# k's first block ahead of x's second quarter, and the second sine table of each pair made from the first one's angles

## The chip, the core and the metric

The kernel runs on one core of a Trainium2 chip. A core has five engines, each with its own instruction queue that is worked off in order: PE (TensorE, matmuls and transposes into PSUM), DVE (VectorE, elementwise), ACT (ScalarE, functions and copies out of PSUM), POOL (GpSimd) and SP (SyncE, which here only issues transfers). They wait for each other through semaphores. Transfers (DMA) are issued by SP, ACT and POOL and run on 16 DMA engines that they share. The metric is the device time of one execution in microseconds.

## The reference, cut to what matters

Two independent halves share one output of 2048 rows. A: a sliding, dilated attention of 32 heads (window 8, dilation 2). B: a short shift filter over k of four taps, a product with v, a long convolution with a filter per channel, a gate with q.

```python
# A: x [2048, 576]
q, k, v = split(x @ wqkv)                  # 32 heads of 18
logits = q . k[pos - 2*w], w = 0..7        # masked where pos - 2*w < 0
o = softmax(logits * 18**-0.5) . v[pos - 2*w]
a = o @ wo
# B: q, k, v [2048, 576]
k_shift[s] = sum_t k_pad[s + t] * shift_k[:, 3 - t]      # k_pad: three zero rows, then k
kv = k_shift * v
y = irfft(rfft(kv, 2S) * rfft(ssm_k, 2S))[:S] + kv * ssm_D
b = q * y
out = concatenate([a, b], axis=-1)
```

## The kernel before, in words

The instructions stand in the program in an order written out by hand; no scheduler moves them. What is issued first on an engine runs first on it. Only the big part in the middle draws "units" of PE work from a list, and that list too is fixed when the program is built.

**Loads.** The order of the calls is the order on SP's queue: x's first quarter (`load_x(0)`, line 194), a third of wqkv for q (`load_w`, lines 154 and 156), x's second quarter (`load_x(1)`, line 194), k's first block of 512 rows (`load_k(0)`, lines 210 and 213), the third of wqkv for k, v's first block, k's second block, x's last two quarters by transposing transfers (`turn_x`), and so on. `load_k(0)` issues six transfers on SP: for rows 3 to 6 of the seven that a partition holds two by line 210 and one by line 213, then the same for rows 0 to 2. The first partition, which needs the three zero rows of the pad, is filled apart: a POOL memset of `kj[0:1, 0:3]` (line 205) and a POOL transfer of four rows (line 206).

**x turned.** The first two quarters of x lie with positions on the partitions and are transposed on PE (lines 467 and 472), then copied out of PSUM by ACT and DVE (lines 527, 528, 538, 477). `project_first(jp, ct0)` (line 494) projects q from quarter jp for two column tiles at a time: eight matmuls at line 500, two at line 502, one copy by ACT at line 504. PE's order around the change is: transposes of the first quarter, `spread_taps(256)`, `project_first(0, 0)`, transposes of the second quarter, `project_first(0, 2)`, `project_first(1, 0)`, `project_first(1, 2)`, then the units: projections of k (lines 378 and 389, copied by ACT at line 414) with folds of kv (line 606), transposes of sine tables (line 455) and others between. All the projections' PSUM tiles have the tag "A", of which there are two buffers: a projection may start when the copy of the one before the last is done.

**Sine tables.** The long convolution is done as products with cosines and sines. DVE makes integer angles: per table pair two multiply-adds (line 438) and one bitwise and (line 439), into `n_all`; ACT turns 1024 angles per partition into bf16 by one Sin (line 440). There are four such calls: `table_k(0)`, `table_k(1)` for the filter's transform (tile `TK`), `table_x(0)`, `table_x(1)` for kv's (tile `TX`). DVE makes the angles of k's two tables before the copies of x's first quarter (line 527), and those of x's two behind them. ACT's sines are placed apart, between the copies of projections:

```python
    project_first(0, 2)
    sines[2]()
    for n in range(2):
        project_first(1, 2 * n)
        sines[3 - 3 * n]()
```

and the fourth, `sines[1]`, behind the second unit (`with_sine`, line 554).

**Taps.** `taps(i)` (line 571) is DVE's work on block i: products of k's rows with the tap weights (line 577), sums (581), the product with v (597). For block 0 the first product reads rows 3 to 6 alone, the second rows 2 to 5. Each block's result is folded on PE (`mirror`, line 606). After the four blocks DVE makes the products of the logits (line 832), which PE sums (line 847) and ACT copies (line 852).

The tile `xw` begins with 512 columns of zeros (DVE memset, line 161) for PE's first idle matmuls (line 178); block 0's first tap product overwrites that place.

Of the kernel before, what the change touches and what calls it, by code (L numbers as in the profile page):

```python
# [11 lines left out]
ACT = mybir.ActivationFunctionType  # L12
ALU = mybir.AluOpType
FP32 = mybir.dt.float32
# [39 lines left out]
def view(t, offset, dims):  # L54

    return bass.AP(tensor=t.tensor, offset=t.offset + offset, ap=[list(t.ap[0])] + [list(d) for d in dims])
# [3 lines left out]
def kernel(  # L60
# [13 lines left out]
    nc = tc.nc  # L74
# [28 lines left out]
    HB = 4 * D  # L103
# [23 lines left out]
    xw = main.tile([128, 12 * HB], BF16, name="xw")  # L127
    XO = 8 * BL
    TB = main.tile([128, XO + 4 * BL], BF16, name="TB")
    TK = view(TB, 0, [[2 * BL, 2], [BL, 2], [1, BL]])  # L130
    TX = view(TB, XO, [[BL, 4], [1, BL]])
# [13 lines left out]
    def w_at(kb, comp):  # L145
        return HB * (9, 10, 5)[comp] + D * kb if kb < 4 else 11 * HB + D * (1, 2, 0)[comp]

    def wq(kb, comp, c0, n):
        return view(xw, w_at(kb, comp) + c0, [[1, n]])

    def load_w(eng, comp, to=None):
        low, high = (to[:, 0:4, :], to[:, 4, :]) if to is not None else \
            (view(xw, w_at(0, comp), [[D, 4], [1, D]]), wq(4, comp, 0, D))
        eng.dma_start(low, A_wqkv[0:512, comp * D:(comp + 1) * D].rearrange("(kb p) a -> p kb a", p=128))
        for r in range(2):
            eng.dma_start(high[64 * r:64 * r + 64, :], A_wqkv[512:576, comp * D:(comp + 1) * D])

    s1 = ExitStack()
    sp1 = s1.enter_context(tc.tile_pool(name="s1", bufs=1, reuse_waits="tile"))
    zeros = view(xw, 0, [[1, 512]])  # L160
    nc.vector.memset(zeros, 0.0)
    pib = main.tile([128, 1], FP32, name="pib")
# [3 lines left out]
    nc.scalar.dma_start(skrow[96:97, :], B_shift_k.rearrange("d j -> (d j)").unsqueeze(0))  # L166
    warm = sp1.tile([128, 1], FP32, name="warm")
    nc.scalar.activation(warm[:], pib[:], ACT.Sin)
    ones96 = sp1.tile([97, 256], BF16, name="ones96")
    nc.vector.memset(ones96[:], 0.0)  # L170
    nc.vector.memset(ones96[96:97, 0:128:2], 1.0)
# [10 lines left out]
    Ks = main.tile([128, 12 * HB], BF16, name="Ks")  # L182
    xnat = view(Ks, 4 * HB, [[HB, 4], [D, 4], [1, D]])
    n_all = view(Ks, 8 * HB, [[1, 4 * HB]]).bitcast(I32).rearrange("p (n f) -> p n f", n=9)
# [8 lines left out]
    def load_x(qtr):  # L193
        nc.sync.dma_start(xnat[:, qtr], xf[512 * qtr:512 * qtr + 512, :].rearrange("(sb p) c -> p sb c", p=128))
# [3 lines left out]
    def load_k(i):  # L198

        eng = nc.sync  # L200
        kj = sp1.tile([128, 7, D], BF16, name="kj", bufs=2)
        r0 = BL * i
        low = [(0, 64)]
        if i == 0:
            nc.gpsimd.memset(kj[0:1, 0:3, :], 0.0)
            nc.gpsimd.dma_start(kj[0:1, 3:7, :], kf[0:4, :].unsqueeze(0))
            low = [(1, 49), (49, 64)]
        for a, b in ((3, 7), (0, 3)) if i == 0 else ((0, 7),):
            for p0, p1 in low:
                eng.dma_start(kj[2 * p0:2 * p1:2, a:b], bass.AP(  # L210
                    tensor=kf.tensor, offset=kf.offset + (r0 + 4 * p0 - 3 + a) * D,
                    ap=[[4 * D, p1 - p0], [D, b - a], [1, D]]))
            eng.dma_start(kj[1:128:2, a:b], bass.AP(tensor=kf.tensor, offset=kf.offset + (r0 + 256 + 3 - a) * D,
                                                    ap=[[4 * D, 64], [-D, b - a], [1, D]]))
        kjs.append(kj)
# [15 lines left out]
    rp = main.tile([128, 8], FP32, name="rp")  # L231
# [10 lines left out]
                            base=0, channel_multiplier=-1)  # L242

    load_w(nc.sync, 0)
    load_x(1)

    def turn_x(h):
# [2 lines left out]
        nc.sync.dma_start(xnat[:, 2 + h, :, 512:576], xf[r0:r0 + 512, 512:576].rearrange("(sb p) c -> p sb c", p=128))  # L250
        nc.sync.dma_start_transpose(view(xw, 6 * HB + 512 * h, [[1024, 4], [1, 512]]), xf[r0:r0 + 512, 0:512])

    load_k(0)
    load_w(nc.sync, 1)
    load_v(0)
    load_k(1)
    turn_x(0)
    turn_x(1)
# [16 lines left out]
    for h in range(2):  # L275
        f = fold[:, 64 * h:64 * h + 64]
# [156 lines left out]
    nc.vector.tensor_copy(rp[:], rp_i[:])  # L433
    nc.vector.tensor_scalar(rp[64:128, 4:8], rp[64:128, 4:8], -510.0, None, op0=ALU.add)

    def table(n_i, T, vec, cols, period, offs):
        for n in range(2):
            nc.vector.tensor_scalar(n_i[:, n, :], vec, rp[:, cols[n]:cols[n] + 1], offs[n], op0=ALU.mult, op1=ALU.add)
        nc.vector.tensor_single_scalar(n_i, n_i, period - 1, ALU.bitwise_and)
        return lambda: nc.scalar.activation(T, n_i, ACT.Sin, bias=pib[:], scale=-2.0 * np.pi / period)  # L440

    def table_k(c):
        return table(n_all[:, 2 * c:2 * c + 2, :], TK[:, c, :, :], n_all[:, 8, :], (2 + c, 2 + c), 2048, (256.0, 1792.0))

    def table_x(n):
        return table(n_all[:, 4 + 2 * n:6 + 2 * n, :], TX[:, 2 * n:2 * n + 2, :], n_all[:, 8, :], (4, 5), 4096,
              (512.0 + 1024.0 * n,) * 2)

    def table_i(s):

# [28 lines left out]
    def pair_x():  # L479
        return pp.tile([128, 2, 1024], BF16, name="ps_x", tag="B")  # L480
# [13 lines left out]
    def project_first(jp, ct0):  # L494

        ps = bank2("ps_proj", "A")
        for e in range(2):
            c0 = 128 * (ct0 + e)
            for kb in range(4):
                nc.tensor.matmul(ps[:, e, :], wq(kb, 0, c0, 128), xT(kb, 512 * jp, 512), start=(kb == 0), stop=False)  # L500
        for e in range(2):
            nc.tensor.matmul(ps[:, e, :], wq(4, 0, 128 * (ct0 + e), 128)[64 * jp:64 * jp + 64],
                             x5(0)[64 * jp:64 * jp + 64], start=False, stop=True, tile_position=(64 * jp, 0))
        nc.scalar.activation(view(q, S * ct0 + 512 * jp, [[S, 2], [1, 512]]), ps[:], ACT.Copy)

    def spread_taps(n0):
        n = min(256, D - n0)
        ps = bank2("ps_sk", "A" if n == 256 else "B")
        for h in range(0, n, 128):
            w = min(128, n - h)  # L510
            sk = skrow[:, 4 * (n0 + h):4 * (n0 + h + w)].rearrange("p (d j) -> p d j", j=4)
            for r in range(2):
                nc.tensor.matmul(ps[:, h // 128, 0:4 * w], ones96[:, 128 * r:128 * r + 128],
                                 sk if r else view(skrow, 4 * (n0 + h) + 3, [[4, w], [-1, 4]]),
                                 start=(r == 0), stop=(r == 1))
        nc.scalar.activation(skb[:, :, n0:n0 + n],
                             ps[:].rearrange("p b (d j) -> p j (b d)", j=4)[:, :, 0:n], ACT.Copy)

    spread_taps(512)
    spread_taps(0)  # L520
    sines = [table_k(0), table_k(1)]
    pts = [pair_x() for _ in range(2)]
    for n in range(2):
        transpose_x(0, pts[n], 2 * n, range(4))
# [3 lines left out]
        nc.scalar.activation(xT(2 + n, 0, 512), pts[1][:, n, 0:512], ACT.Copy)  # L528
    copy_tail(0, pts[1])
    spread_taps(256)  # L530
    sines += [table_x(0), table_x(1)]
    project_first(0, 0)
    pts = [pair_x() for _ in range(2)]
    for n in range(2):
# [125 lines left out]
    def fold_filter(m):  # L660
        kt, swapped = kTok(m), m < 2

        def unit():
            assert m in signed
            minus = minus_of(m)
            pss = [bank2("ps_rev", "A") for _ in range(2)]
            for c in range(2):
                turns = [((flip2r, flip1)[c] if swapped else flip0, 1 - c), ((identn0, identn)[c], 2 + c)]
                if not swapped:
                    turns.insert(1, ((corner2, corner)[c], c))  # L670
                for n, (w, of) in enumerate(turns):
                    for h in range(2):
                        nc.tensor.matmul(pss[c][:, h, 0:HD], w[:], kt[:, of, HD * h:HD * h + HD], start=(n == 0),  # L673
                                         stop=(n == len(turns) - 1))
            for c in range(2):
                nc.scalar.activation(halves(kt[:, c, :]), pss[c][:, :, 0:HD], ACT.Copy, scale=0.5)
                pe(0.5, "A", 0.65)
            nc.gpsimd.dma_start(view(Ks, k_at(m, 2) + 2 * D, [[1, 2 * D]]), view(Ks, k_at(m, 2), [[1, 2 * D]]),
                                accum_op=ALU.add, max_dma_last_dim=2 * D)
            nc.gpsimd.dma_start(other(m)[1:128], kt[1:128, 0, :], accum_op=ALU.add)  # L680
            nc.gpsimd.dma_start(other(m)[0:1], minus, accum_op=ALU.add)

        return (1.0, unit, f"fold{m}")
# [21 lines left out]
    def made(f, *args):  # L705
        n = len(units)
        f(*args)
        return [units.pop() for _ in range(len(units) - n)][::-1]
# [13 lines left out]
    for i in range(NBL):  # L722
# [4 lines left out]
        if i < 2:  # L727
            load_k(i + 2)
            load_v(i + 2)
# [14 lines left out]
        if i == 3:  # L744
            need("fold3")
            first = made(filter_spectrum, 3)
            now = deque(first)
            first = [[now.popleft() for _ in range(min(n, len(now)))] for n in EARLY]
            now, first = first[0] + [fold_filter(2)] + first[1] + mirrors[:1] + first[2] + mirrors[1:], list(now)
# [3 lines left out]
        for n, u in enumerate(mirrors):  # L753
            n = AT[n] if n < 2 else AT[i]
# [591 lines left out]
```

## Time and profile before

| what | us |
|---|---|
| median of 3 runs | 212.61 |
| lowest and highest | 212.39 and 212.65 |
| the profiled execution | 212.5 |
| its span in the profile | 210.8 |

The profile shows one execution. Times within it count from the start of the span, which is 1.7 us shorter than the execution. A row of the timeline gives start, duration, engine, line, operation, what is written from what, and how many instructions were merged; in brackets stands how long the engine idled before and what ended the wait. SPq stands for an issue of a transfer on SP, PEld for a weight load. The chain of waits is the work that ended last, followed back from the end. In the slices a digit is the busy share in tenths of one fortieth of the span. A DMA's time to landing counts from its issue.

### The profile page before, as it was taken

The numbers are of one execution on the slowest core, as the hardware profiler recorded it, in microseconds if no ns is written. First come the engines' busy times: TensorE is split into PE (matmuls) and PEld (weight loads), VectorE is DVE, ScalarE is ACT, GpSimd is POOL, SyncE is SP. The second block draws the span as 40 slices with busy tenths as digits, with TensorE's granted clock in tenths as the row PEclk, the third lists the DMA queues.
The fourth block names the chain that finished last, engine by engine and source line by source line (L and its number), as shares of the span: only waits on it lengthen the run. The fifth ranks groups of instructions, "written<-read, shape, count | busy, mean of one in ns | idle before, by whom it ended". The sixth has DMA issues, their size and how long they took to land.

```text
span 210.8 us, 5106 instructions
## 1 busy us (share of the span) xinstructions
PE 200.1 (95%) x2114; PEld 110.7 (53%) x2122; DVE 193.1 (92%) x146; ACT 150.5 (71%) x218; POOL 74.0 (35%) x111
## 2 busy tenths in 40 slices
PE   7999999999999999899999999999989999999891
PEld 2443443344554656564354666656555666666460
DVE  7989999999999999858889999999999849999981
ACT  3799988657684989986369788855666796775540
POOL 8999993001195516320175000002029004033000
PEclk9999999999999999999999999999999999999999
DMA  6999998999639336999999997587559995985133
GB/s 201 303 328 231 266 342 280 170 192 182 151 75 122 48 40 87 180 181 171 235 225 238 194 234 159 105 208 185 153 223 255 239 322 110 214 243 182 28 113 111
DMA packets 35396, 39.66 MB, mean 188 GB/s; under 512 B 17619, under 2 KB 29007, under 8 KB 35374
## 3 DMA queue, kind: packets, MB, share of 16 engines
q1 hardware_dynamic: 26812, 24.88, 47.2%
q0 software_dynamic: 6096, 11.96, 30.4%
q10 hardware_dynamic: 2466, 2.51, 3.5%
q8 instruction: 16, 0.26, 0.5%
q14 instruction: 6, 0.05, 0.1%
HBM read 13.11 MB, written 4.72 MB: 85 GB/s over the span
## 4 chain that ended last, share of the span: by engine, by line
PE 80%; ACT 10%; DVE 5%; issue 2%; DVEq 0%; ACTq 0%
PE ps_proj L378 16%; PE ps_z L1126 9%; PE ps_wo L1029 8%; PE ps_acc L973 7%; PE ps_inv L1158 7%; PE ps_fx L776 6%; PE ps_log L847 4%; PE ps_proj L500 3%; PE ps_fk L627 3%; PE ps_proj L382 3%; PE ps_proj L389 3%; ACT Ks L695 3%; PE ps_rev L673 2%; PE ps_fk L628 1%; ACT qk L977 1%
## 5 line engine op out<-in xcount | busy, mean ns | idle before, releaser
L378 PE MATMUL ps_proj<-xw 128*128 128x512 bf16 x153 | 37.4, 380 | 0.6 <-issue 0.3
L832 DVE TENSOR_TENSOR av<-qk 128x4096 bf16<-128x4096 bf16 (+1 forms) x16 | 31.7, 2013 | 2.8 <-PE ps_log L847 2.8
L378 PEld LDWEIGHTS <-xw 128*128 128x128 bf16 x160 | 14.0, 97 | 20.5 <-issue 6.2
L1099 DVE TENSOR_TENSOR qk<-xw,Ks 128x2304 bf16<-128x2304 bf16 x14 | 18.5, 1355 | 2.5 <-PE ps_inv L1158 2.4
L1139 ACT ACTIVATE av<-ps_z 128x768 bf16<-128x768 f32 x20 | 15.3, 808 | 6.2 <-PE ps_z L1126 6.2
L414 ACT ACTIVATE qk<-ps_proj 128x1024 bf16<-128x1024 f32 x14 | 14.3, 1023 | 7.6 <-PE ps_proj L389 3.3
L695 ACT ACTIVATE Ks<-ps_fk 128x576 bf16<-128x576 f32 x32 | 18.6, 717 | 1.3 <-PE ps_fk L628 1.3
L577 DVE TENSOR_TENSOR tB<-kj,skb 128x4608 bf16<-128x4608 bf16 (+1 forms) x8 | 19.3, 2417 | 0.1
L778 ACT ACTIVATE xw<-ps_fx 128x576 bf16<-128x576 f32 x32 | 18.4, 666 | 0.0
L776 PE MATMUL ps_fx<-xw,TB 128*128 128x288 bf16 x128 | 18.0, 286 | 0.2
L1055 POOL DMA_DIRECT2D Ks<-Ks x3 | 3.7, 1218 | 41.1 <-PE ps_wo L1029 28.7
L1029 PE MATMUL ps_wo<-qk 128*128 128x288 bf16 x128 | 17.8, 287 | 0.0
L627 PE MATMUL ps_fk<-Ks,TB 128*128 128x384 bf16 x62 | 16.9, 326 | 0.8 <-ACT Ks L695 0.7
L414 ACT ACTIVATE v<-ps_proj 128x1024 bf16<-128x1024 f32 x9 | 9.3, 1029 | 9.3 <-PE ps_proj L378 4.3
L973 PE MATMUL ps_acc<-av,ident 64*64 64x512 bf16 x160 | 15.3, 377 | 0.0
L628 PE MATMUL ps_fk<-Ks,TB 128*128 128x192 bf16 x62 | 15.2, 245 | 0.0
L776 PEld LDWEIGHTS <-TB 128*128 128x128 bf16 x128 | 12.0, 97 | 6.0 <-issue 2.9
L1029 PEld LDWEIGHTS <-qk 128*128 128x128 bf16 x128 | 11.6, 98 | 5.6 <-issue 3.0
L1158 PE MATMUL ps_inv<-av,TI 128*128 128x288 bf16 (+1 forms) x96 | 13.6, 293 | 0.6 <-ACT av L1139 0.6
L1161 ACT ACTIVATE v<-ps_inv 128x576 bf16<-128x576 f32 (+1 forms) x14 | 9.5, 677 | 6.3 <-PE ps_inv L1158 6.3
L977 ACT ACTIVATE qk<-ps_acc 128x1024 bf16<-128x1024 f32 x8 | 8.2, 1024 | 8.0 <-PE ps_acc L973 8.0
L956 DVE TENSOR_TENSOR av<-Ks,v 128x4096 bf16<-128x4096 bf16 x6 | 13.6, 2286 | 0.2 <-PE ps_acc L973 0.2
(199 smaller groups left out, 471.3 us busy)
## 6 DMA issues: line engine op xcount, KB each, us to landing
Ks<-Ks POOLq DMA_DIRECT2D x9, 576.0 KB, 7.1
TB<-av SPq DMA_DIRECT2D x12, 256.0 KB, 5.5
kj<-in_B_k_dram SPq DMA_DIRECT2D x6, 504.0 KB, 6.1
vt<-in_B_v_dram SPq DMA_DIRECT2D x8, 288.0 KB, 5.2
Ks<-av SPq DMA_DIRECT2D x8, 256.0 KB, 5.5
Ks<-Ks SPq DMA_DIRECT2D x3, 576.0 KB, 6.1
Ks<-in_A_x_dram SPq DMA_DIRECT2D x2, 576.0 KB, 5.2
xw<-in_A_wqkv_dram SPq DMA_DIRECT2D x2, 576.0 KB, 5.9
```

What stands on the lines that cost most here:

```text
L378: nc.tensor.matmul(ps[:, jp, :], wq(kb, comp, 128 * ct, 128), xT(kb, 1024 * jj + 512 * jp, 512), **se)
L414: nc.scalar.activation(view(t, o + pad + 1024 * jj, [[512, 2], [1, 512]]), ps[:], ACT.Copy)
L577: dve(2304 * n, lambda: nc.vector.tensor_tensor(to, view(kj, row * D, [[D, n], [D, 4], [1, D]]), view(skb, row * D, [[D, n], [0, 4], [1, D ...
L627: nc.tensor.matmul(o[:, 0:2], w, rhs[:, 0:2], start=start, stop=stop)
L695: nc.scalar.activation(view(Ks, k_at(m, cs ^ (m & 1)) + 96 * gi, [[768, 3], [384, 2], [1, 96]]), acc3(ps), ACT.Copy, scale=(PSG, MSG)[cs][ ...
L776: nc.tensor.matmul(ps[:, pm, 0:HD], TX[:, 2 * pm + c, 128 * gi:128 * gi + 128], kv[:, 2 * c + pm, HD * h:HD * h + HD], start=(c == 0), sto ...
L832: return P, at, step, dve(1024 * nj, lambda: nc.vector.tensor_tensor(view(P, at, [[step, 4], [256, nj], [1, 256]]), view(t, o + 256 * hh, ...
L973: nc.tensor.matmul(acc[64 * o:64 * o + 64, h, :], ident[64 * h:64 * h + 64, 64 * h:64 * h + 64], view(P, 256 * u, [[2048, 2], [1, 256]])[6 ...
L1029: nc.tensor.matmul(ps[:, r, 0:HD], oT(hh, 2 * c + r, t)[:, o:o + 128], wo[:, t // 2, t % 2, HD * h:HD * h + HD], start=(t == 0 and h == 0) ...
L1099: r = dve(3 * QTR, lambda: nc.vector.tensor_tensor(pr, view(xw, HB * XG[i] + QTR * t, [[HB, 3], [1, QTR]]), view(Ks, k_at(j - i, 0) + QTR ...
L1126: nc.tensor.matmul(view(acc[r], 512 * h, [[192, 2], [96, 2], [1, 96]])[o:o + 64], w[64 * h:64 * h + 64, 64 * h:64 * h + 64], pr[64 * h:64 ...
L1158: nc.tensor.matmul(ps[:, c, 0:n], TI[:, sl, pm, 128 * c:128 * c + 128], Y(j, pm)[:, sl, c0:c0 + n], start=(pm == 0 and sl == 0), stop=(sl ...
```

## The change

Three edits. The call `load_k(0)` moves ahead of `load_x(1)`. Each pair of sine tables is made from one set of angles: ACT takes the Sin of the first table from the integer angles as before, then the absolute value of the same argument (Abs, into an fp32 place that the second table's integers had), and later the second table as the Sin of that value, scaled by plus or minus one and shifted by a quarter turn held in a new one-column tile. So DVE makes angles twice and not four times, and ACT does six calls and not four: `sines` now holds Sin and Abs of k's tables, the second Sin of k's, Sin and Abs of x's, the second Sin of x's, called at the same four places. And the three zero rows ahead of k are brought by a transfer on ACT's queue from the zeros in `xw` in place of a POOL memset.

```diff
+    quarter_turn = {}
+    for sign in (-1, 1):
+        quarter_turn[sign] = sp1.tile([128, 1], FP32, name="quarter_turn", bufs=2)
+        nc.gpsimd.memset(quarter_turn[sign][:], float(np.float32(-0.5 * sign * np.pi)))
...
         if i == 0:
-            nc.gpsimd.memset(kj[0:1, 0:3, :], 0.0)
+            nc.scalar.dma_start(kj[0:1, 0:3, :], view(xw[0:1], 0, [[0, 4], [1, 432]]))
             nc.gpsimd.dma_start(kj[0:1, 3:7, :], kf[0:4, :].unsqueeze(0))
...
     load_w(nc.sync, 0)
+    load_k(0)
     load_x(1)
...
-    load_k(0)
     load_w(nc.sync, 1)
...
-    def table(n_i, T, vec, cols, period, offs):
+    def table(at, cols, period, off, T, sign):
+        n_i = n_all[:, at:at + 2, :]
         for n in range(2):
-            nc.vector.tensor_scalar(n_i[:, n, :], vec, rp[:, cols[n]:cols[n] + 1], offs[n], op0=ALU.mult, op1=ALU.add)
+            nc.vector.tensor_scalar(n_i[:, n, :], n_all[:, 8, :], rp[:, cols + n:cols + n + 1], off, op0=ALU.mult,
+                                    op1=ALU.add)
         nc.vector.tensor_single_scalar(n_i, n_i, period - 1, ALU.bitwise_and)
-        return lambda: nc.scalar.activation(T, n_i, ACT.Sin, bias=pib[:], scale=-2.0 * np.pi / period)
...
+        mag = view(Ks, 8 * HB, [[1, 4 * HB]]).bitcast(FP32).rearrange("p (n f) -> p n f", n=9)[:, at + 2:at + 4, :]
+
+        def first():
+            nc.scalar.activation(T[0], n_i, ACT.Sin, bias=pib[:], scale=-2.0 * np.pi / period)
+            nc.scalar.activation(mag, n_i, ACT.Abs, bias=pib[:], scale=-2.0 * np.pi / period)
+
+        def second():
+            nc.scalar.activation(T[1], mag, ACT.Sin, bias=quarter_turn[sign][:], scale=float(sign))
+
+        return [first, second]
+
+    def table_k():
+        return table(0, 2, 2048, 256.0, [TK[:, :, n, :] for n in range(2)], -1)
+
+    def table_x():
+        return table(4, 4, 4096, 512.0, [TX[:, 2 * n:2 * n + 2, :] for n in range(2)], 1)
...
-    sines = [table_k(0), table_k(1)]
+    sines = table_k()
...
-    sines += [table_x(0), table_x(1)]
+    sines += table_x()
```

More of the change, by code (lines that the diff above doesn't have):

```diff
@@ L434 @@
     nc.vector.tensor_scalar(rp[64:128, 4:8], rp[64:128, 4:8], -510.0, None, op0=ALU.add)
-    def table(n_i, T, vec, cols, period, offs):
+    def table(at, cols, period, off, T, sign):
+        n_i = n_all[:, at:at + 2, :]
         for n in range(2):
-            nc.vector.tensor_scalar(n_i[:, n, :], vec, rp[:, cols[n]:cols[n] + 1], offs[n], op0=ALU.mult, op1=ALU.add)
+            nc.vector.tensor_scalar(n_i[:, n, :], n_all[:, 8, :], rp[:, cols + n:cols + n + 1], off, op0=ALU.mult,
+                                    op1=ALU.add)
         nc.vector.tensor_single_scalar(n_i, n_i, period - 1, ALU.bitwise_and)
[L440 to L447, printed above, removed]
+        mag = view(Ks, 8 * HB, [[1, 4 * HB]]).bitcast(FP32).rearrange("p (n f) -> p n f", n=9)[:, at + 2:at + 4, :]
[9 more added lines that the diff above has]
+        return table(4, 4, 4096, 512.0, [TX[:, 2 * n:2 * n + 2, :] for n in range(2)], 1)
     def table_i(s):
```

## The prediction

> **What bounds the kernel now.** I read the page's busy times, slices and chain first, then the chain in order of time, then the waits of DVE, then the timelines of SP, PE, DVE and ACT up to 26 us, where all of the change lies.
>
> ```profile
> PE 200.1 (95%) x2114; PEld 110.7 (53%) x2122; DVE 193.1 (92%) x146; ACT 150.5 (71%) x218; POOL 74.0 (35%) x111
> ...
> PE   7999999999999999899999999999989999999891
> ...
> DVE  7989999999999999858889999999999849999981
> ...
> PE 80%; ACT 10%; DVE 5%; issue 2%; DVEq 0%; ACTq 0%
> ```
>
> Two engines look full, and the chain decides between them: 80% of it is PE, 5% DVE. The slices say where DVE gives way. It is full up to the sixteenth and then drops to 5 to 8 tenths, while PE stays at 9 but for one 8. Ten microseconds at a time (columns: PE, PEld, DVE, ACT, POOL), and DVE's longest wait:
>
> ```profile
> 80.00:90.00 10.00, 9.24 (x80) 5.75 (x82) 8.82 (x7) 10.00 (x17) 4.63 (x5) 1.00 0.90 146
> 90.00:100.00 10.00, 9.84 (x84) 5.32 (x78) 7.20 (x5) 7.59 (x13) 1.17 (x1) 1.00 1.02 175
> 100.00:110.00 10.00, 9.84 (x75) 4.01 (x75) 8.65 (x6) 4.86 (x5) 4.81 (x9) 1.00 0.95 228
> ```
>
> ```profile
> DVE av L832 <- PE ps_log L847: 2.8, 3, 1.4
> ```
>
> Between 80 and 110 us DVE idles 1.2 + 2.8 + 1.4 = 5.3 us, and its longest wait there is for PE's sums of the logits. So a few microseconds won on DVE before 80 us only lengthen that wait, and the time follows PE, whose instructions stand in one fixed order. In the first 26 us PE meets two edges, and the change touches both.
>
> **First part: the order of the loads.** load_k(0) issues six transfers on SP, one on POOL and, now, one on ACT. Between the old and the new place of the call POOL and ACT issue nothing, so only SP's order changes: the six pass one transfer, x's second quarter.
>
> ```profile
> 3.13 0.59 SPq L194 DMA_DIRECT2D Ks<-in_A_x_dram  x1
> 3.76 1.54 SPq L210 DMA_DIRECT2D kj<-in_B_k_dram  x2
> 5.35 0.73 SPq L213 DMA_DIRECT2D kj<-in_B_k_dram  x1
> 6.12 1.58 SPq L210 DMA_DIRECT2D kj<-in_B_k_dram  x2
> 7.75 0.66 SPq L213 DMA_DIRECT2D kj<-in_B_k_dram  x1
> 8.46 0.60 SPq L154 DMA_DIRECT2D xw<-in_A_wqkv_dram  x1
> ```
>
> The six begin at 3.76 and the next load at 8.46: 4.70 us of SP. The quarter, now issued at 3.13, is issued at 3.13 + 4.70 = 7.83. The transfers from line 194 and from line 213 took, from issue to landing:
>
> ```profile
> DMA to landing us min/median/max: 4.2/5.2/6.2
> ...
> DMA to landing us min/median/max: 5.1/6.3/6.9
> ```
>
> ```profile
> 7.80 1.91 PE L500 MATMUL ps_proj<-xw 128*128 128x512 bf16 x8 [0.35 <-DVE xw L527]
> 9.65 0.60 PE L502 MATMUL ps_proj<-xw 64*128 64x512 bf16 x2
> 10.18 1.07 PE L467 MATMUL ps_x<-ident,Ks 128*128 128x128 bf16 x16
> ...
> 11.88 1.36 DVE L577 TENSOR_TENSOR xw<-kj,skb 128x2304 bf16<-128x2304 bf16 x1 [0.72 <-DMA kj<-in_B_k_dram]
> ...
> 13.15 1.36 DVE L577 TENSOR_TENSOR tB<-kj,skb 128x2304 bf16<-128x2304 bf16 x1
> ```
>
> The quarter has landed by 3.13 + 6.2 = 9.33 today, 0.85 us ahead of its transposes at 10.18. When does it land in its new place? By the two transfers of line 194, between 7.83 + 4.2 = 12.0 and 7.83 + 6.2 = 14.0. The nearest row is another: k's last piece is today the eleventh transfer of SP, issued at 7.75, behind the same bytes that the quarter will have ahead of and in it. It landed no earlier than 7.75 + 5.1 = 12.85 (the shortest of its line), and by 13.24, when the second tap product, which reads it, follows the first (11.88 + 1.36) without a wait. I take 13.05. PE has nothing else in its order: the second pair of first projections stands behind the transposes. So PE starts them at 13.05 in place of 10.18: **2.87 us later**, with bounds of 1.8 and 3.8. ACT's copies of the transposed quarter, and all behind them, move by as much.
>
> In exchange k lands earlier by about the quarter's share of the queue, some 2 us: the first tap product starts near 10 in place of 11.88. That is a gain for DVE, which the wait of the 90s takes back: nothing.
>
> **Second part: the sine tables.** DVE loses two of the four tables:
>
> ```profile
> L438 DVE TENSOR_SCALAR Ks<-Ks,rp 128x512 int32<-128x512 int32 x8 | 3.6, 494 | 0.0
> ...
> L439 DVE TENSOR_SCALAR Ks<-Ks 128x1024 int32<-128x1024 int32 x4 | 2.8, 709 | 0.1
> ...
> L440 ACT ACTIVATE TB<-Ks,pib 128x1024 bf16<-128x1024 int32 x4 | 4.6, 1140 | 0.0
> ```
>
> Half of 3.6 + 2.8 is 3.2 us less on DVE before 11.1. Without it the taps would still wait for k. What it reaches on PE is the start of the first projection, which waited 0.35 us for a DVE copy at 7.80; those 0.35 us end in the wait for x's quarter: nothing. ACT keeps its four sines and gains two Abs of 128x1024, one behind the first sine and one behind the third. The trace has no Abs. Its nearest row is the sine of the same shape and input, 1.14 us; the cheapest of this size is a copy at 1.02. ACT is full at this place:
>
> ```profile
> 14.21 1.02 ACT L504 ACTIVATE qk<-ps_proj 128x1024 bf16<-128x1024 f32 x1
> 15.13 1.14 ACT L440 ACTIVATE TB<-Ks,pib 128x1024 bf16<-128x1024 int32 x1
> 16.36 1.02 ACT L504 ACTIVATE qk<-ps_proj 128x1024 bf16<-128x1024 f32 x1
> 17.28 1.14 ACT L440 ACTIVATE TB<-Ks,pib 128x1024 bf16<-128x1024 int32 x1
> 18.73 1.02 ACT L504 ACTIVATE qk<-ps_proj 128x1024 bf16<-128x1024 f32 x1 [0.30 <-PE ps_proj L502]
> 19.65 1.14 ACT L440 ACTIVATE TB<-Ks,pib 128x1024 bf16<-128x1024 int32 x1
> 20.89 1.02 ACT L414 ACTIVATE qk<-ps_proj 128x1024 bf16<-128x1024 f32 x1
> 21.81 1.14 ACT L440 ACTIVATE TB<-Ks,pib 128x1024 bf16<-128x1024 int32 x1
> 22.93 1.02 ACT L414 ACTIVATE qk<-ps_proj 128x1024 bf16<-128x1024 f32 x1
> ```
>
> ```profile
> 22.95 1.01 ACT qk L414
> ...
> 24.00 0.38 PE ps_proj L378
> ```
>
> From start to start a sine takes 1.12 us where nothing lies between (21.81 to 22.93). So the slack behind the first three sines is 16.36 - 16.25 = 0.11, then 18.73 - 18.40 = 0.33, then 20.89 - 20.77 = 0.12, in all 0.56 us. Two Abs at 1.12 are 2.24; less the slack, the copy at 22.93 comes 1.68 us later. The last two rows, from the chain, show who waits: PE's projection at 24.00 starts when that copy (22.95 + 1.01) has emptied its PSUM buffer. PE therefore loses **1.68 us** a second time. Bounds: at a copy's pitch of 0.92 (14.21 to 15.13) 1.84 - 0.56 = 1.28; with no overlap and no slack 2 x 1.14 = 2.28. Both losses add, since ACT's row as a whole moves with the transposes.
>
> The trace shows no load of another function table beside the sines. [...]
>
> **Third part: k's pad by a transfer.** POOL loses a memset and gains two of one column; ACT gains one issue.
>
> ```profile
> L205 POOL MEMSET kj<- 1x1728 bf16 x1 | 1.5, 1529 | 0.0
> ...
> 3.62 0.38 ACT L516 ACTIVATE skb<-ps_sk 128x256 bf16<-128x256 f32 x1 [0.73 <-PE ps_sk L513]
> ```
>
> POOL is 1.5 us ahead; no engine above waits for it. ACT's issue stands where ACT idles 0.73 us before 3.62, and what it reads, DVE's zeros, is long there. An issue of 0.5 to 0.9 us, as SP's rows show, fits or comes 0.2 us late to a copy that leads to the taps alone: nothing. Its landing, at most 6.2 us on, is before 10. If it came later only DVE's first products would wait.
>
> **The sum.** 2.87 + 1.68 = 4.55 us on PE before 29 us, with no part of it given back that the chain shows: it stays on PE or on ACT behind PE. The profiled execution took 212.5 us (span 210.8, 1.7 around it), the median is 212.61. 212.5 + 4.55 = 217.05, with the 0.1 to the median **217.1 us**. From the bounds alone: 1.8 + 1.28 gives 215.7, 3.8 + 2.28 gives 218.7.
>
> **The rivals.** (1) *The quarter lands in time all the same*, since transfers share 16 engines and mine treats them as a queue: ACT's term alone, 212.6 + 1.7 = 214.3. Against it: no transfer of these lines lands in under 4.2 us. 8%. (2) *The Abs hide*, in the wait for x: 212.6 + 2.9 = 215.5. Against it: ACT's order puts them behind the copies of that x. 12%. (3) *PE's clock falls* during the wait. The row that prices it:
>
> ```profile
> L178 PE MATMUL ps_idle<-xw 128*128 128x512 bf16 x4 | 1.9, 627 | 1.3 <-DVE pib L163 1.3
> ...
> 5.08 1.06 PE L467 MATMUL ps_x<-ident,Ks 128*128 128x128 bf16 x16
> ```
>
> The first matmuls took 1.9 / 4 = 0.47 us each, where eight of that shape took 1.91 at 7.80; the transposes at 5.08 are as fast as those at 10.18 (1.06 and 1.07). So PE started at half speed and was full by 5.08, at most 3.8 us on. Going through that again would cost half of 3.8: 217.1 + 1.9 = 219.0. The wait of 3.1 us (from 9.65 + 0.60 - 0.35 = 9.9 to 13.05) is the first long one behind it; the trace has no such wait to show what the clock does. [...] 10%. (4) *The Abs bring table loads*, one before and one behind each: four at the 1.28 us of
>
> ```profile
> L168 ACT ACT_TABLE_LOAD x1 | 1.3, 1283 | 1.4 <-PEq L1330 1.4
> ```
>
> add 5.1: 222.2. 3%. (5) *Faster: DVE is the bound after all.* From 11.88 to 80 us DVE has hardly a wait, so its 1.9 us of earlier taps would pass through to the end: 210.7. It decides only if x's quarter lands by 10.2, so that PE stays ahead, and if the logits' products then hold up the sums and not the reverse. The waits of the 90s speak against it. 4%. (6) *All of it hides*, within 0.2%: 3%.
>
> **How the numbers follow.** The forecast of both terms has 60%. Slower by over 0.2% (0.4 us, about what a measurement of this kernel can tell from no change) are the forecast and rivals 1 to 4: 0.93; within it 0.03; faster 0.04. The range from 214.2 to 219.1 takes in rivals 1 to 3 and the bounds, and leaves out some 13 in 100: rivals 4 to 6 and a tail.
>
> **What would show it.** Step one: the transposes of x's second quarter start near 13 with a wait for the transfer of x, and the tap products near 10. Step two: Abs rows of about 1.1 us, and PE waiting for a copy of line 414's kind near 28.5. Sum: the sums of the logits and all behind them later by 4 to 5 us, DVE's idle time before 110 us longer by 5 or more. I am wrong if the transposes start before 12, if PE's wait at the second edge is missing, or if PE makes the loss good where DVE now leads.

## The result, and the profile after

The changed kernel takes 217.91 us (median of 4 runs, 217.13 to 221.53) against 212.55 us before; the ratio is 1.0246, 95% interval 1.0219 to 1.0274. The run of 221.53, whose mean granted clock was 0.94, is not in the ratio; without it the median is 217.25. The profiled execution took 217.25 us, 4.75 more than the one profiled before, its span is 215.5 against 210.8.

The page of the changed kernel, the same parts as shown of before:

```profile
PE 201.9 (94%) x2114; PEld 112.2 (52%) x2122; DVE 189.4 (88%) x140; ACT 152.1 (71%) x220; POOL 68.2 (32%) x112
...
PE   7959989999999999989999999999989999999891
...
DVE  6599999999952999966889999999999959899982
...
PE 76%; ACT 13%; DMA 5%; issue 2%; DVE 1%; SPq 1%; DVEq 0%; ACTq 0%
```

DVE has 3.7 us less work and a new hole in its twelfth and thirteenth slice (5 and 2 tenths). PE has a hole in its third (5), and a transfer now stands in the chain with 5%. PE's instructions are as many as before, yet it is busy 1.8 us *longer*, which the diff does not explain. Here are PE's timeline at the first hole, SP's issues ahead of it, and the time to landing of line 198, the loads of x:

```profile
9.76 0.60 PE L516 MATMUL ps_proj<-xw 64*128 64x512 bf16 x2
12.89 1.59 PE L481 MATMUL ps_x<-ident,Ks 128*128 128x128 bf16 x16 [2.53 <-DMA Ks<-in_A_x_dram]
...
15.80 1.89 PE L514 MATMUL ps_proj<-xw 128*128 128x512 bf16 x6 [0.22 <-issue]
17.63 0.60 PE L516 MATMUL ps_proj<-xw 64*128 64x512 bf16 x2
```

```profile
5.61 2.22 SPq L214 DMA_DIRECT2D kj<-in_B_k_dram  x2
7.88 0.66 SPq L217 DMA_DIRECT2D kj<-in_B_k_dram  x1
8.59 0.60 SPq L198 DMA_DIRECT2D Ks<-in_A_x_dram  x1
```

```profile
DMA to landing us min/median/max: 4.2/4.2/4.3
```

PE waits 2.53 us for x's second quarter and starts on it at 12.89, 2.71 us later than before. Then it is slow: the 16 transposes take 1.59 us (1.07 before), and the last two matmuls of the projection start at 17.63 where before they started at 13.36, so 2.71 has become 4.27. The granted clock (the third number from the right in a row of one microsecond, before the DMA share and the GB/s) says why:

```profile
13.00:14.00 1.00, 1.00 (x14) 1.00 (x14) 1.00 (x1) 0.00 (x0) 1.00 (x1) 0.63 1.10 384
14.00:15.00 1.00, 1.00 (x10) 0.63 (x8) 0.96 (x2) 0.00 (x0) 1.00 (x2) 0.50 1.05 333
15.00:16.00 1.00, 0.78 (x3) 0.41 (x4) 1.00 (x1) 0.92 (x1) 1.00 (x1) 0.50 1.20 371
16.00:17.00 1.00, 1.00 (x4) 0.36 (x3) 0.96 (x2) 1.00 (x2) 0.94 (x2) 0.66 0.96 381
17.00:18.00 1.00, 1.00 (x6) 0.21 (x3) 0.99 (x1) 0.61 (x2) 1.00 (x1) 1.00 0.95 341
```

It falls to one half at about 13.26 (0.26 at full and 0.74 at half speed make 0.63) and is back at 16.68. The wait is the first loss and the clock the second. The third is the place where PE waits for ACT ("ACT's edge" below). These are ACT's sine, Abs and copy, then the copy that PE needs, and PE itself:

```profile
19.19 1.14 ACT L449 ACTIVATE TB<-Ks,pib 128x1024 bf16<-128x1024 int32 x1
20.23 1.14 ACT L450 ACTIVATE Ks<-Ks,pib 128x1024 f32<-128x1024 int32 x1
21.27 1.01 ACT L518 ACTIVATE qk<-ps_proj 128x1024 bf16<-128x1024 f32 x1
...
28.14 1.03 ACT L418 ACTIVATE qk<-ps_proj 128x1024 bf16<-128x1024 f32 x1
```

```profile
29.22 1.02 PE L382 MATMUL ps_proj<-xw 128*128 128x512 bf16 x3 [0.99 <-ACT qk L418]
```

An Abs takes 1.14 us, 1.04 from start to start. PE waits 0.99 us for the copy, and its third unit starts at 29.22 in place of 24.00: 5.22 late. From there PE keeps that distance: each of its sums of the logits, products with v and inverse transforms starts 5.20 or 5.21 us later than before, up to what stood at 194 us. DVE's rows, the first from before, the others from the changed kernel:

```profile
56.70 4.47 DVE L832 TENSOR_TENSOR av<-qk 128x4096 bf16<-128x4096 bf16 x2
```

```profile
9.97 1.36 DVE L591 TENSOR_TENSOR xw<-kj,skb 128x2304 bf16<-128x2304 bf16 x1 [1.51 <-DMA kj<-in_B_k_dram]
...
54.95 4.47 DVE L846 TENSOR_TENSOR av<-qk 128x4096 bf16<-128x4096 bf16 x2
...
68.82 3.43 DVE L846 TENSOR_TENSOR av<-qk 128x4096 bf16<-128x4096 bf16 x2 [6.76 <-ACT v L418]
```

The taps begin at 9.97 (11.88 before), the products of the logits at 54.95 (56.70 before), and then DVE waits 6.76 us for ACT's copy of what PE projected late. Its lead is wholly given back there; up to 110 us DVE is busy 8.3 us less than before, of which 3.7 are work that it no longer has. Only at the very end is something won back. The chain before, then after:

```profile
192.13 1.12 issue
193.25 0.91 DVE qk L1099
194.16 0.36 issue
```

```profile
200.17 1.10 PE ps_z L1140 x24
201.27 0.02 issue
201.29 0.82 ACT av L1153
```

Before, the last stage of PE stood for a moment behind DVE; now DVE comes in time, and the distance falls from 5.21 to 4.80.

### The profile page after: what moved, and what is told of

Same layout as the page of the kernel before. It is cut to its first block, busy times and chain, and to the rows that moved or that the text cites. A ratio compares the mean times of both kernels' runs of the same rounds, so it can differ in the third digit from the quotient of the medians.

```text
span 215.5 us, 5105 instructions
## 1 busy us (share of the span) xinstructions
PE 201.9 (94%) x2114; PEld 112.2 (52%) x2122; DVE 189.4 (88%) x140; ACT 152.1 (71%) x220; POOL 68.2 (32%) x112
## 4 chain that ended last, share of the span: by engine, by line
PE 76%; ACT 13%; DMA 5%; issue 2%; DVE 1%; SPq 1%; DVEq 0%; ACTq 0%
PE ps_proj L382 15%; PE ps_z L1140 9%; PE ps_wo L1043 8%; PE ps_inv L1172 7%; PE ps_acc L987 7%; PE ps_fx L790 6%; PE ps_log L861 4%; PE ps_fk L641 3%; DMA xw<-in_A_wqkv_dram 3%; ACT Ks L709 3%; PE ps_proj L386 3%; PE ps_proj L393 2%; DMA Ks<-in_A_x_dram 2%; PE ps_rev L687 2%; PE ps_fk L642 1%
```

## The experiments

**Theory:** PE sets the time, and loses it in three places: by the wait for x (load order), by the clock that falls during or behind that wait, and by ACT's edge (the Abs). **Rivals:** the tables or the transfers alone carry the loss; DVE sets the time; PE was slow because transfers disturb it, not by its clock.

**The load order alone.** The kernel before, with

```diff
     load_w(nc.sync, 0)
+    load_k(0)
     load_x(1)
```

and the old call taken out.

> The kernel before with the load order of the changed one alone (k's first block ahead of x's second quarter; tables and pad as before). Theory (PE waits for x's quarter, then runs at half clock for a while): the transposes of x's second quarter start at 12.6 to 12.9 in place of 10.18, the tap products near 10; PE's projections of the units are 4.0 to 4.4 us later where the clock falls and 2.5 to 2.8 where it does not, the wait before the copy of line 414 near 24 adds under 0.2. Time 216.2, between 214.8 and 216.8. Rival (the tables carry the loss): 212.6 to 213.5.

216.1 us (median of 4; 214.73, 216.0, 216.19, 216.31) against 212.38, ratio 1.0163 [1.0136, 1.0190]. The median is as expected; the profiled run is the one at 214.73:

```profile
12.80 1.07 PE L467 MATMUL ps_x<-ident,Ks 128*128 128x128 bf16 x16 [2.55 <-DMA Ks<-in_A_x_dram]
...
26.62 1.89 PE L378 MATMUL ps_proj<-xw 128*128 128x512 bf16 x7
```

The wait is there (2.55 us), the transposes are fast, and the third unit is 2.62 late. So the same wait does not always cost the clock. The three other runs left no profile, so the same kernel was run once more.

> The new load order alone once more, for a second profile. Theory: if the time is near 216.1, the granted clock is under 1.00 for some 3.4 us from 12.9 to 14 us on, the matmuls of the projection behind the transposes take twice as long, and the units are 4.0 to 4.2 us later than before; if the time is near 214.7 the clock is 1.00 throughout and the units are 2.6 us later. Rival: near 216.1 with a clock of 1.00.

216.38 us in one run, and this profile shows the fall:

```profile
12.79 1.07 PE L467 MATMUL ps_x<-ident,Ks 128*128 128x128 bf16 x16 [2.02 <-DMA Ks<-in_A_x_dram]
...
14.13 3.57 PE L500 MATMUL ps_proj<-xw 128*128 128x512 bf16 x8
```

```profile
14.00:15.00 1.00, 1.00 (x7) 0.37 (x5) 1.00 (x1) 0.76 (x1) 0.99 (x1) 0.60 1.01 272
15.00:16.00 1.00, 1.00 (x4) 0.39 (x3) 0.97 (x2) 1.00 (x2) 0.89 (x3) 0.50 1.19 422
16.00:17.00 1.00, 1.00 (x3) 0.30 (x2) 1.00 (x1) 0.77 (x2) 1.00 (x1) 0.50 0.94 370
17.00:18.00 1.00, 1.00 (x4) 0.11 (x2) 0.96 (x2) 0.00 (x0) 0.93 (x2) 0.69 1.00 337
```

The transposes start at the same place (12.79 and 12.80) and take 1.07 us in both. Here the clock falls at 14.2, behind them, and the eight matmuls of the projection take 3.57 us in place of 1.90. The units' first projection starts at 22.91 here and at 21.24 there, 1.67 us apart, for 1.65 between the two times.

**The wait filled.** If the clock falls because PE idles, giving it work must stop that. Eleven matmuls whose result nobody reads, in the changed kernel and in the kernel with the order alone:

```diff
     project_first(0, 0)
+    ps = bank2("ps_idle", "A")
+    for _ in range(11):
+        nc.tensor.matmul(ps[:, 0, :], wq(0, 0, 0, 128), wq(0, 0, 0, 512), start=True, stop=True)
```

> The changed kernel with 11 matmuls of 512 columns on q's weights, whose result nobody reads, between the first projection and the transposes of x's second quarter: PE is busy in place of idle while it waits. Theory (the wait lets PE's clock fall): granted clock 1.00 in 13 to 17 us, the 16 transposes in 1.07 us in place of 1.59, the eight matmuls of the projection behind them in 1.9 in place of 2.7; ACT's edge behind takes back 0.2 of the 1.56. Time 215.9, between 215.5 and 216.4. Rival (PE is slow there since the transfers disturb its reads): no change against the changed kernel, 217.2.

215.94 us (215.91 to 216.10), ratio 1.0171 [1.0155, 1.0186]: the useless work makes the changed kernel over a microsecond faster, and its runs agree within 0.2 us. The transposes take 1.07 us again, and ACT's edge takes back its part, 1.20 us:

```profile
12.83 1.07 PE L481 MATMUL ps_x<-ident,Ks 128*128 128x128 bf16 x16 [0.62 <-DMA Ks<-in_A_x_dram]
...
27.81 1.89 PE L382 MATMUL ps_proj<-xw 128*128 128x512 bf16 x7 [1.20 <-ACT qk L418]
```

> The kernel before with the new load order alone, and 11 matmuls of 512 columns on q's weights between the first projection and the transposes of x's second quarter. With the order alone the profiled execution kept its full clock through a wait of 2.55 us and took 214.73 us, while the three other runs took 216.0 to 216.3. Theory (in those runs the clock fell in the wait): with PE busy all runs lie near 214.7, between 214.4 and 215.0, without the runs at 216. Rival (the 1.4 us come from elsewhere, such as the transfers): runs at both levels as before, median 216.1.

214.87 us (214.56 to 215.00), ratio 1.0101 [1.0057, 1.0145]: no run at 216 any more. The transposes still start at 12.88, for x comes no earlier and the transfers are the same ones; only PE's idling is gone, and with it the slow matmuls. So a disturbance by the transfers is out as the cause.

**The tables alone.** The kernel before with the new `table` and its calls; loads and pad as before.

> The kernel before with the new sine tables alone (load order and pad as before). Theory (ACT is full between 14 and 23 us, two Abs of 1.04 each less the slack of some 0.9): PE's projection of the third unit starts 0.9 to 1.3 us late, less 0.3 won where the first projection no longer waits for DVE's copy. Time 213.2, between 212.8 and 213.6. Rival A (the Abs hide): 212.3. Rival B (DVE is the bound, and 3.2 us less on it shorten the kernel): under 211.5.

213.29 us (212.69 to 214.0, 8 runs), ratio 1.0043 [1.0027, 1.0059]: slower, though DVE is busy 2.9 us less (190.2 for 193.1). PE's wait at the third unit is 1.21 us:

```profile
25.22 1.89 PE L382 MATMUL ps_proj<-xw 128*128 128x512 bf16 x7 [1.21 <-ACT qk L418]
```

**The Abs twice.** The same, with

```diff
             nc.scalar.activation(mag, n_i, ACT.Abs, bias=pib[:], scale=-2.0 * np.pi / period)
+            nc.scalar.activation(mag, n_i, ACT.Abs, bias=pib[:], scale=-2.0 * np.pi / period)
```

> The kernel before with the new sine tables, and each of the two Abs issued twice (same result). Theory (ACT sets PE's pace here with no slack left): two more Abs of 1.04 us come through in full, PE's wait before the third unit is 1.2 + 2.1 = 3.3 us, time 213.3 + 2.1 = 215.4, between 215.0 and 215.8; more by up to 1.5 if PE's clock falls in that wait. Rival (the loss of the tables lies elsewhere, such as the strided table or DVE): 213.3 as with one.

215.38 us (215.08 to 217.2), ratio 1.0161 [1.0127, 1.0196]; 2.1 us over one Abs each, as expected. PE's waits for ACT's copies up to 40 us:

```profile
PE ps_proj L382 <- ACT qk L418: 1.3, 1, 1.3
...
PE ps_ti L470 <- ACT qk L418: 1.2, 1, 1.2
PE ps_proj L382 <- ACT qk L519: 0.8, 1, 0.8
```

They sum to 3.3 us, 2.1 over the 1.2 of one Abs. There is no slack left on ACT at this place: what is added comes through whole.

**The pad alone.**

```diff
-            nc.gpsimd.memset(kj[0:1, 0:3, :], 0.0)
+            nc.scalar.dma_start(kj[0:1, 0:3, :], view(xw[0:1], 0, [[0, 4], [1, 432]]))
```

> The kernel before with k's pad by a transfer alone. Theory: DVE's cast of line 433, 1.07 us beside POOL's memset, falls to 0.1, so the copies of x's first quarter and the first projection start 0.3 us earlier, which PE keeps: 212.3, between 212.0 and 212.6. SP's fourth transfer of k waits for q's weights, as in the changed kernel (7.0 us), so what follows on SP is 0.5 to 1 us later and costs nothing. Rival (the later issues reach PE): 213.0 or more.

212.44 us (212.19 to 214.49, 12 runs), ratio 1.0003 [0.9979, 1.0027]: no difference that these runs show. PE does get its start, and loses it:

```profile
7.35 1.89 PE L500 MATMUL ps_proj<-xw 128*128 128x512 bf16 x8
...
22.90 0.68 PE L606 MATMUL ps_fold<-xw,fold 128*64 128x288 bf16 x8 [0.48 <-DVE xw L597]
```

It begins the first projection 0.45 us earlier and at 22.90 waits 0.48 us for block 0's product on DVE. So DVE, though not the bound, stands right behind PE there.

> The kernel before with the pad by a transfer, and the two folds of block 0 one pair of units later on PE. With the pad alone PE ran 0.46 us ahead from 7.4 us on and lost it at 22.9, waiting 0.48 us for DVE's product that the first fold reads. Theory: with the fold behind the next projection PE keeps its lead; 0.3 to 0.46 us less than before: 212.0, between 211.9 and 212.3. Rival (the lead is lost at the next edge, ACT's copies, or by the fold's copies coming late): no change, 212.4.

Pad by transfer and `n = AT[n] + 2 * (i == 0) if n < 2 else AT[i]`, so that the fold comes a pair of units later: 212.61 us (212.05 to 214.61, 12 runs) against 212.25, ratio 1.0015 [0.9994, 1.0035]. The wait for DVE is gone; in its place PE waits for ACT:

```profile
5.11 1.90 PE L467 MATMUL ps_x<-ident,Ks 128*128 128x128 bf16 x16
...
30.82 1.46 PE L378 MATMUL ps_proj<-xw 128*128 128x512 bf16 x6 [0.49 <-ACT TI L459]
```

The rival's edge is there. The first row shows an execution whose clock rose late (1.90 us for transposes that take 1.07 at full clock), so this profile cannot say how much of the lead lived until 30.8; the runs show no gain. No version here beats the kernel before.

**PE's own work in the wait.** In the changed kernel, `project_first(0, 2)` ahead of the transposes of x's second quarter.

> The changed kernel with the second pair of first projections ahead of the transposes of x's second quarter, so that PE has 2.37 us of its own work where it waited. Theory: PE waits under 0.7 us for x's quarter and its clock stays full, but the projection behind the transposes now waits for ACT's two copies of the quarter (1.94 us), so 1 to 2 us of the loss come back in another place; ACT's edge adds 0.5 to 1. Time 215.0, between 214.0 and 216.0. Rival A (the wait for x is the whole of the loss): 213.4. Rival B (order on PE makes no difference): 217.2.

215.58 us (215.09 to 216.4), ratio 1.0157 [1.0132, 1.0182], within the theory's range and off in one part:

```profile
12.87 1.07 PE L481 MATMUL ps_x<-ident,Ks 128*128 128x128 bf16 x16 [0.69 <-DMA Ks<-in_A_x_dram]
...
15.39 3.63 PE L514 MATMUL ps_proj<-xw 128*128 128x512 bf16 x8 [1.11 <-ACT xw L553]
```

The wait for x shrinks to 0.69 us and, as expected, 1.11 us come back as a wait for ACT's copies of the quarter. The expectation that the clock would stay full was wrong: it fell at 15.5, just behind the second of these two waits, and the projection took 3.63 us in place of 1.9. This profiled execution, at 216.4 us, is the slowest of the four.

## Why the prediction was right, point by point

- **What bounds the kernel.** Right. DVE started its logits 1.75 us earlier and then waited 6.76 us; PE's delay of 5.2 us passed through 165 us of the kernel unchanged.
- **x's second quarter.** Right in its result: transposes at 12.89 for a forecast of 13.05, 2.71 us for 2.87. The way there was a little different: it was issued at 8.59 and not at 7.83, since SP waited 0.8 us, until 7.02, for the load of q's weights. With the order alone, where the pad is a memset, SP does not stand there and issues the quarter at 7.74; with the pad alone it does. PE could start at nearly the same time either way (12.80 and 12.89), so the time of issue did not set the landing. That the bytes ahead of it did, as the choice of the nearest row assumed, fits both; no run varied them alone.
- **The Abs.** Mechanism right, size too high: 1.68 forecast, 1.20 and 1.21 measured with the clock full, 0.99 in the changed kernel, where ACT's copies came only 4.06 us later (18.27 for 14.21) and PE 4.27, which is 0.21 us more of slack. The step that failed took the sine's pitch as 1.12 from the starts at 21.81 and 22.93, "where nothing lies between". The copy at 22.93 had waited for PE, whose matmuls ended at 22.89. The pitch is 1.04 in the changed kernel. With it the four gaps between sine and copy in the rows of before are 0.19, 0.41, 0.20 and 0.08, in all 0.88 us, and 2.08 - 0.88 is the 1.20 that was measured. No table was loaded around the Abs: in the changed kernel an Abs follows its sine after 1.04 us, and the trace has two table loads of 1.28 us, at 1.40 and 38.46 us (before: at 1.39 and 33.31), none of them between the first sine at 19.19 and the last at 27.10.
- **The clock.** This was a rival at 10% and it happened in the profiled execution, and probably in the other two at 217.13 and 218.56, whose mean granted clocks are no higher (0.989 and 0.984, for 0.990). It cost 4.27 - 2.71 = 1.56 us, for a price of 1.9. So a loss that the forecast left out of its sum was there. The 10% was the author's estimate: the trace of before, in which PE waits 1.3 us at most, could not show what a longer wait does. In the changed kernel PE idled 2.53 us and the clock fell (more below).
- **The sum.** 4.55 us forecast, 4.75 measured in the profiled execution, by errors that cancel: 0.16 too much for the load, 0.69 too much for the Abs, 1.56 missed for the clock, and 0.41 given back at the end, where "no part of it given back" was wrong. (These four make 4.85; the 0.1 that is left lies in PE's gaps and behind its last matmul.) Two of the three losses were foreseen with their mechanism; that the total came so close, without the third, is luck. By the ratio the loss is 5.2 us.
- **The pad at nothing.** Right for this kernel, for half the reason: POOL's memset did cost something, since DVE's small cast (line 433, 437 after the change) took 1.07 us beside it and takes 0.10 in the changed kernel. PE's 0.45 us behind that are real but lost again at the first fold. In the changed kernel they do not show, since its clock rose late and the first projection started at 7.94, behind the 7.80 of before.

## What to carry to other kernels

An engine with a fixed order pays for a late input at once, and for good when it is the bound: here PE paid 2.71 us for x's quarter. The lead of 1.75 us that DVE won, an engine that waits for it, was worth nothing. Work moved to an engine that is full just there costs its duration less the gaps at that place (1.20 of 2.08 us for the first two Abs, all of the next two), however much slack that engine has over the whole span, so weigh it in the stage where it lands. When taking a pitch from two starts, first see whether the second instruction was waiting for someone.

## What the runs showed of the hardware

PE's clock fell after waits shorter than the time for which it then stayed low, and not always after the same wait. It fell after 2.53 us of idle time in the changed kernel, after 2.02 us in the second run of the load order, and after 0.69 and 1.11 us close together in the kernel with the projections swapped. It did not fall after 2.55 us in the first run of the load order, nor after 0.62 us with the wait filled.

The granted clock was one half from 13.26 to 16.68 us in the changed kernel, from 14.2 to 17.6 in the second run of the load order, and from 15.5 to 18.9 with the projections swapped, 3.4 us each time. The rows of the last:

```profile
15.00:16.00 1.00, 0.61 (x2) 0.25 (x2) 1.00 (x1) 1.00 (x2) 1.00 (x1) 0.76 1.22 358
16.00:17.00 1.00, 1.00 (x3) 0.25 (x2) 0.97 (x2) 0.95 (x3) 1.00 (x2) 0.50 0.98 380
17.00:18.00 1.00, 1.00 (x4) 0.33 (x3) 1.00 (x1) 1.00 (x2) 1.00 (x1) 0.50 0.93 342
18.00:19.00 1.00, 1.00 (x4) 0.16 (x3) 0.96 (x2) 1.00 (x2) 0.88 (x8) 0.54 1.13 325
```

The changed kernel and the first run of the load order had nearly the same wait, 2.53 us before 12.89 and 2.55 us before 12.80, and only the changed kernel lost its clock there. The two executions already differ ahead of that wait, in the transposes of x's first quarter, which take 1.07 us at the full clock:

```profile
5.09 1.70 PE L481 MATMUL ps_x<-ident,Ks 128*128 128x128 bf16 x16
```

```profile
5.04 1.07 PE L467 MATMUL ps_x<-ident,Ks 128*128 128x128 bf16 x16
```

What decides whether the clock falls in a wait was not shown; no run was made to find it. With PE busy in the wait it stayed full: in the profile of the changed kernel with the wait filled it is 1.00 in every row from 10 to 19 us, and with the load order and the wait filled the transposes take 1.07 us and the eight matmuls behind them 1.90.
